# One output tile in three indirect transfers of 256 columns, and 30 identity matmuls at the start in place of 36

## Chip, cores and metric

The kernel runs on one core of a Trainium2 chip. The metric is the device time of one execution in microseconds (us); of several executions the median is given. The core has five engines that work side by side and meet at semaphores: TensorE (PE, matrix multiply; its weight loads are shown as PEld), VectorE (DVE), ScalarE (ACT), GpSimd (POOL) and SyncE (SP), and 16 DMA engines that move bytes between the chip's main memory and the on-chip memories.

## What is computed

Three stages follow one another. Attention over 2 batches, 12 heads, 448 positions and 64 columns per head gives 896 tokens of 768 columns. A mixture of 8 experts then sends each token through the one expert that its logits choose. Last comes a dense part, and it alone matters for the end of the kernel.

```python
def _moe2_ref(x, w1, w2, w3, w_out):
    h = np.maximum(np.maximum(x @ w1, x @ w2), x @ w3)
    return (h @ w_out).astype(np.float32)

def reference(...):
    x = attention(q, k, v)                     # (896, 768)
    x = _moe_ref(x, expert_emb, tau, w1, w2)   # one expert of 8 for each token
    return _moe2_ref(x, moe2_w1, moe2_w2, moe2_w3, moe2_w_out)   # (896, 768), float32
```

## The kernel before, in words

The order of the instructions on each engine is the order in which the program writes them; a framework puts in the semaphore waits that its view of the data needs. Every float32 product is made of three matmuls on two halves of each operand (`mm3`, lines 974 to 977).

**The start.** Lines 99 to 101 build the identity matrix `ident` and its 16-bit copy `identb` on POOL. Line 700 loads the keys and queries of the first head pair, and lines 703 to 705 run 36 matmuls of `identb` with itself (128 columns each) into a bank `warm` that nobody reads. Then the attention schedule begins: the keys `kt` of a pair are scaled on DVE (line 479), the scores go to PE (line 500), a mask is added by matmul (line 506), the row maximum is taken on DVE (line 510) and the exponential on ACT (line 517).

**The middle.** The tokens are sorted by expert, so that blocks of 128 rows use one expert's weights. `sorted_table2` (lines 970 to 972), which runs at the end of slot 1 (the second block of rows), inverts the sort with 16 small matmuls into a bank `ix` and casts seven columns of it into the integer table `sidx`. Column t of `sidx` holds, for each of the 128 rows of output tile t, the row of `out` that it belongs to.

**The end.** Seven output tiles of 128 rows and 768 columns are made in the loop over t (line 1102). Each has two parts n: the first 384 columns and the last 384, for the last tile 512 and 256 (line 1104). For each part 18 matmuls fill a bank `po`; ACT copies the first part into the tile `ob` (line 1110) and DVE the second (line 1112). After both, line 1113 scatters the whole tile with one indirect DMA that POOL issues; each row goes to the row of `out` that `sidx` names:

```python
nc.gpsimd.indirect_dma_start(out=out, out_offset=bass.IndirectOffsetOnAxis(ap=sidx[:, t:t + 1], axis=0), in_=ob, in_offset=None)
```

The buffers for `ob` alternate between two pools (line 1103). Line 1154 is the end of the program, where SP waits for all semaphores and the engines meet.

Of the kernel before, what the change touches and what calls it, by code (L numbers as in the profile page):

```python
# [10 lines left out]
I32 = mybir.dt.int32  # L11
AF = mybir.ActivationFunctionType
ALU = mybir.AluOpType
# [23 lines left out]
def kernel(  # L37
# [15 lines left out]
    nc = tc.nc  # L53
    B, H, S, D = 2, 12, 448, 64
    N, DM = out.shape
    E = emb.shape[0]
    P = 128
# [8 lines left out]
    const = ctx.enter_context(tc.tile_pool(name="const", bufs=1))  # L66
# [18 lines left out]
    def bank(tag, name, bufs=None):  # L85
        return ps.tile([P, 512], F32, tag=tag, name=name, bufs=bufs)

    V = nc.vector
# [175 lines left out]
    def mm3(o, lh, ll, rh, rl, first, last):  # L264
        nc.tensor.matmul(o, lhsT=lh, rhs=rh, start=first, stop=False)
        nc.tensor.matmul(o, lhsT=lh, rhs=rl, start=False, stop=False)
        nc.tensor.matmul(o, lhsT=ll, rhs=rh, start=False, stop=last)
# [199 lines left out]
    held = {}  # L467
# [233 lines left out]
    er, es, esq, table = embed(eb)  # L701
    consts(eb)
    warm = bank("h", "warm", 1)
    for n in range(36):
        nc.tensor.matmul(warm[:, :P], lhsT=identb, rhs=identb, start=True, stop=True)
    load(1)
    loadv(0)
# [144 lines left out]
    def invert(ns):  # L852
        ix = held["ix"] = bank("a", "ix")
        for c in range(NB):
            for t in range(2):
                nc.tensor.matmul(ix[:, :ns], lhsT=A[:, c], rhs=pay[:, t, c, :ns], start=(c + t == 0), stop=(c + t == NB))
# [90 lines left out]
    }  # L947

    sidx = const.tile([P, NB - 1], I32, name="sidx")

    def sorted_table():
        TT(rks[:, 4:], rks[:, 4:], padv[:TB].unsqueeze(1).to_broadcast([TB, 4, E]), ALU.subtract)
        TT(pre8, tri, n8.unsqueeze(1).to_broadcast([P, E, E]), ALU.mult)
        red(tb8, pre8)
        TT(ro, rks, tb8[:TB].unsqueeze(1).to_broadcast([TB, NB, E]), ALU.add)
        TT(ro, ro, oh, ALU.mult)
        red(rr, ro)
        TT(ge, rr.unsqueeze(2).to_broadcast([TB, NB, 6]), k128[:TB, 1:7].unsqueeze(1).to_broadcast([TB, NB, 6]), ALU.is_ge)
        red(sl, ge)
        V.scalar_tensor_tensor(out=jj, in0=sl, scalar=-128.0, in1=rr, op0=ALU.mult, op1=ALU.add)  # L960
        s7 = sel[:, :, :7]
        TT(s7, sl.unsqueeze(2).to_broadcast([TB, NB, 7]), i14[:TB, :7].unsqueeze(1).to_broadcast([TB, NB, 7]), ALU.is_equal)
        TT(pay[:, 0, :, :7], s7, bval[:TB].unsqueeze(2).to_broadcast([TB, NB, 7]), ALU.mult)
        V.tensor_scalar(out=pay[:, 1, :, :7], in0=s7, scalar1=pval[:TB], scalar2=None, op0=ALU.mult)
        onehot(0, 8)
        TT(flg, flg, tabf[:, NS:2 * NS], ALU.mult)
        red(tabf[:, 0:1], flg, ALU.max)
        V.tensor_copy(out=tabi[:, 3 * NS:], in_=tabf[:, 0:1])

    def sorted_table2():  # L970
        invert(7)
        V.tensor_copy(out=sidx, in_=held["ix"][:, :7])

    def mm3(o, lh, ll, rh, rl, first, last):
        nc.tensor.matmul(o, lhsT=lh, rhs=rh, start=first, stop=False)  # L975
# [13 lines left out]
    def rest_hint(i, *engines):  # L989
        tc.mark_branch_hint_location(f"rest{i}", (rest["n"] + (NS - i)) // 16, engines=engines)  # L990

    hooks = {(1, 0): sorted_table, (1, 1): sorted_table2, (5, 1): rest_load}
    for i in range(7, NS):
        hooks[i - 1, 0] = lambda i=i: rest_hint(i, ET.PE, ET.Pool, ET.SP)
# [63 lines left out]
    for m in range(KD):  # L1058
        t0 = [do.tile([P, S], F32, tag=f"t0{b}", name=f"t0{b}", bufs=1) for b in range(2)]
        wraw[m] = None  # L1060
        for a in range(3):
# [12 lines left out]
            else:  # L1074
                c = a - 1
# [26 lines left out]
    for t in range(N // P):  # L1102
        ob = (do, io_p)[t % 2].tile([P, DM], F32, tag="ob", name="ob")
        w = 512 if t == N // P - 1 else 384
        for n, (c0, c1) in enumerate(((0, w), (w, DM))):
            pb = bank("ab"[n], f"po{n}")[:, :c1 - c0]
            for k in range(KD):
                mm3(pb, hh[k // 3][:, k % 3, t * P:(t + 1) * P], hl[:, k, t * P:(t + 1) * P], woh[k][:, c0:c1], wol[k][:, c0:c1], k == 0, k == KD - 1)
            if n == 0:
                nc.scalar.copy(out=ob[:, :c1], in_=pb)  # L1110
            else:
                nc.vector.tensor_copy(out=ob[:, c0:], in_=pb)  # L1112
        nc.gpsimd.indirect_dma_start(out=out, out_offset=bass.IndirectOffsetOnAxis(ap=sidx[:, t:t + 1], axis=0), in_=ob, in_offset=None)  # L1113


_INS = ["q", "k", "v", "moe_expert_emb", "moe_tau", "moe_w1", "moe_w2", "moe2_w1", "moe2_w2", "moe2_w3", "moe2_w_out"]
# [42 lines left out]
```

## Time and profile before

| | |
|---|---|
| median of 3 runs | 478.21 us (477.86 to 478.9) |
| profiled execution, its own time | 477.87 us |
| its span (first to last instruction) | 476.2 us |
| PE busy | 462.1 us, 97% of the span |
| DVE, ACT, POOL busy | 322.7, 267.4, 81.0 us |

The span is what the trace shows; some 1.7 us of the execution lie around it. Times in a trace are counted from the start of the span. An engine's busy time says how much it did and not whether anybody waited for it; what bounds the end is read from the chain of work that ended last and from the instructions near that end.

### The profile page before, as it was taken

The page shows a single profiled execution, that of the slowest core. Times are in us where ns is not written, and L with a number is a line of the kernel's source. Part 1 is how long each engine was busy: PE and PEld are TensorE (multiplying, and loading weights), DVE is VectorE, ACT ScalarE, POOL GpSimd, SP SyncE. Part 2 cuts the span into 40 slices and gives each one's busy share as a digit, 9 for nine tenths or more (in the row PEclk, how much of TensorE's full clock was granted, in tenths as well). Part 3 has the DMA queues.
Part 4 walks back from the last instruction along what each step waited for, and adds up shares of the span by engine and source line. Part 5 has one row for each costly group of instructions (what it writes and reads, how often), then busy time and mean ns, then how long its engine had stood idle before and what let it go on. Part 6 is the DMA issues. An engine that isn't in the chain of part 4 may idle for free. (4 is left out here: it accounts for less than half of the span.)

```text
span 476.2 us, 9239 instructions
## 1 busy us (share of the span) xinstructions
PE 462.1 (97%) x3158; PEld 410.6 (86%) x3158; DVE 322.7 (68%) x650; ACT 267.4 (56%) x560; POOL 81.0 (17%) x103
## 2 busy tenths in 40 slices
PE   8999999899999999999999999999999999999994
PEld 6787768688899998998998987899999999999993
DVE  4999999968444895111977945898988979740000
ACT  6898979867726895234988955444435344310000
POOL 4868474620010000000000000000000000001111
PEclk9999999999999999999999999999999999999999
DMA  8734229441158890119799805754435220000111
GB/s 270 248 123 151 74 63 409 189 132 47 35 179 321 295 355 13 34 54 376 258 343 347 350 2 187 290 181 145 139 127 200 89 111 1 1 0 34 66 67 66
DMA packets 18173, 75.85 MB, mean 159 GB/s; under 512 B 2360, under 2 KB 5432, under 8 KB 18112
## 3 DMA queue, kind: packets, MB, share of 16 engines
q1 hardware_dynamic: 15408, 65.05, 38.3%
q0 software_dynamic: 2400, 9.83, 5.5%
q8 instruction: 26, 0.43, 0.4%
q10 hardware_dynamic: 304, 0.25, 0.2%
q14 instruction: 35, 0.29, 0.2%
HBM read 69.62 MB, written 5.51 MB: 158 GB/s over the span
## 5 line engine op out<-in xcount | busy, mean ns | idle before, releaser
L975 PE MATMUL pm<-x2h,dwh 128*128 128x448 f32 x204 | 75.1, 368 | 0.0
L976 PE MATMUL pm<-x2l,dwh 128*128 128x448 f32 x204 | 75.0, 368 | 0.0
L977 PE MATMUL pm<-x2h,dwl 128*128 128x448 f32 x204 | 74.6, 366 | 0.0
L981 PE MATMUL l<-w2h,hh 128*128 128x384 f32 x160 | 54.9, 343 | 0.7 <-ACT hh L207 0.7
L242 DVE TENSOR_TENSOR w1l<-raw,w1h 128x768 fp32r<-128x768 f32 x40 | 36.0, 950 | 27.8 <-PE l L981 20.5
L981 PE MATMUL l<-w2l,hh 128*128 128x384 f32 x160 | 53.7, 336 | 0.2 <-DVE w2l L262 0.2
L981 PE MATMUL l<-w1h,xhp 128*128 128x512 f32 x109 | 43.8, 402 | 0.0
L981 PE MATMUL l<-w1l,xhp 128*128 128x512 f32 x109 | 42.7, 392 | 0.0
L975 PEld LDWEIGHTS pm<-x2h,dwh 128*128 128x128 f32 x204 | 38.2, 187 | 3.9
L977 PEld LDWEIGHTS pm<-x2h,dwl 128*128 128x128 f32 x204 | 38.3, 188 | 3.7
L517 ACT ACTIVATE prb<-pss,sm 128x64 f32<-128x64 f32 (+6 forms) x84 | 39.2, 492 | 4.1 <-DVE sm L510 3.0
L174 ACT CAST dwh<-dt_t 128x768 fp32r<-128x768 f32 (+1 forms) x20 | 15.5, 773 | 46.2 <-DVE dt_t L173 46.1
L976 PEld LDWEIGHTS pm<-x2l,dwh 128*128 128x128 f32 x204 | 38.3, 188 | 3.4
L1113 POOL DMA_INDIRECT out_dram<-ob,sidx x7 | 6.8, 978 | 198.2 <-DVE ob L1112 198.2
L527 POOL TENSOR_SCALAR prb<-prb,sm 128x64 f32<-128x64 f32 (+6 forms) x38 | 36.0, 964 | 20.8 <-DVE sm L523 19.8
L198 POOL DMA_INDIRECT xrp<-xd,idx x11 | 11.3, 1028 | 152.9 <-PE xtp L216 143.2
L981 PE MATMUL l<-w2h,hl 128*128 128x384 f32 x160 | 36.3, 336 | 0.1
L242 DVE TENSOR_TENSOR w2l<-raw,w2h 128x768 fp32r<-128x768 f32 x40 | 35.1, 946 | 0.0
L204 DVE TENSOR_TENSOR hl<-htp,hh 128x512 fp32r<-128x512 f32 x17 | 11.7, 689 | 31.8 <-ACTq L351 17.8
L510 DVE TENSOR_REDUCE sm<-pss 128x1 f32<-128x128 f32 (+6 forms) x84 | 29.9, 411 | 3.5 <-PE pss L506 3.0
L241 ACT CAST w2h<-raw 128x768 fp32r<-128x768 f32 x40 | 30.5, 839 | 2.3 <-SPq L351 1.6
L241 ACT CAST w1h<-raw 128x768 fp32r<-128x768 f32 x40 | 31.7, 854 | 0.0
(255 smaller groups left out, 1023.9 us busy)
## 6 DMA issues: line engine op xcount, KB each, us to landing
raw<-in_moe_w_dram SPq DMA_DIRECT2D x48, 768.0 KB, 6.3
rawd<-in_moe_w_dram SPq DMA_DIRECT2D x18, 768.0 KB, 4.9
rawd<-in_moe_w_out_dram SPq DMA_DIRECT2D x6, 768.0 KB, 4.4
vr<-in_v_dram SPq DMA_DIRECT2D x12, 256.0 KB, 3.7
kt<-in_k_dram SPq DMA_DIRECT2D x12, 224.0 KB, 3.9
xd<-x2T POOLq DMA_DIRECT2D x12, 224.0 KB, 3.4
qt<-in_q_dram SPq DMA_DIRECT2D x11, 224.0 KB, 3.5
qt<-in_q_dram ACTq DMA_DIRECT2D x1, 224.0 KB, 4.0
```

The costliest lines, as they stand in the source:

```text
L174: nc.scalar.copy(out=hi[:, c0:c1], in_=f)
L198: nc.gpsimd.indirect_dma_start(out=xrp, out_offset=None, in_=xd if i else xd[0:S], in_offset=bass.IndirectOffsetOnAxis(ap=idx[:, i:i + 1] ...
L204: nc.vector.tensor_tensor(out=lo, in0=ps_ap, in1=hi, op=ALU.subtract)
L241: nc.scalar.copy(out=hi[:, sl], in_=r[:, sl])
L242: nc.vector.tensor_tensor(out=lo[:, sl], in0=r[:, sl], in1=hi[:, sl], op=ALU.subtract)
L510: nc.vector.tensor_reduce(out=sms[p][:, 0, SC[i]:SC[i] + 1], in_=held["s", p, g][:, SO[i]:SO[i] + 64 * (i + 1)], axis=AX.X, op=ALU.max, ne ...
L517: nc.scalar.activation(out=prb[p % 2][:, poff[i]:poff[i] + n], in_=ps[:, SO[i]:SO[i] + n], func=AF.Exp, bias=sm[:, 0, SC[i]:SC[i] + 1], sc ...
L527: eng.tensor_scalar(out=r, in0=r, scalar1=sms[p][:, 2, SC[i]:SC[i] + 1], scalar2=None, op0=ALU.mult)
L975: nc.tensor.matmul(o, lhsT=lh, rhs=rh, start=first, stop=False)
L976: nc.tensor.matmul(o, lhsT=lh, rhs=rl, start=False, stop=False)
L977: nc.tensor.matmul(o, lhsT=ll, rhs=rh, start=False, stop=last)
L981: nc.tensor.matmul(o, lhsT=a, rhs=b, start=first and n == 0, stop=last and n == len(ops) - 1)
```

## The change

The warm-up loop issues 30 matmuls. `sorted_table2` makes, beside `sidx`, a second integer table `sidx3` of three columns: three times the row number of the last tile, plus 0, 1 and 2. With `out` seen as 2688 rows of 256 columns, these are the rows at which the three thirds of an output row begin. The scatter moves into the loop over n: tiles 0 to 5 are still written whole after their second part; of the last tile two transfers of 256 columns follow its first part (512 columns) and one its second part.

```diff
-    for n in range(36):
+    for n in range(30):
         nc.tensor.matmul(warm[:, :P], lhsT=identb, rhs=identb, start=True, stop=True)
...
     sidx = const.tile([P, NB - 1], I32, name="sidx")
+    sidx3 = const.tile([P, 3], I32, name="sidx3")
...
     def sorted_table2():
         invert(7)
         V.tensor_copy(out=sidx, in_=held["ix"][:, :7])
+        for c in range(3):
+            V.tensor_scalar(out=sidx3[:, c:c + 1], in0=held["ix"][:, 6:7], scalar1=3.0, scalar2=float(c), op0=ALU.mult, op1=ALU.add)
...
-        nc.gpsimd.indirect_dma_start(out=out, out_offset=bass.IndirectOffsetOnAxis(ap=sidx[:, t:t + 1], axis=0), in_=ob, in_offset=None)
+            if t == N // P - 1:
+                for c in (2,) if n else (0, 1):
+                    nc.gpsimd.indirect_dma_start(out=out.rearrange("n (c d) -> (n c) d", c=3), out_offset=bass.IndirectOffsetOnAxis(ap=sidx3[:, c:c + 1], axis=0), in_=ob[:, 256 * c:256 * c + 256], in_offset=None)
+            elif n:
+                nc.gpsimd.indirect_dma_start(out=out, out_offset=bass.IndirectOffsetOnAxis(ap=sidx[:, t:t + 1], axis=0), in_=ob, in_offset=None)
```

## Rows read from the trace of the kernel before

**Rows 1.** The page: busy time, share of the span and instructions of each engine.
```profile
PE 462.1 (97%) x3158; PEld 410.6 (86%) x3158; DVE 322.7 (68%) x650; ACT 267.4 (56%) x560; POOL 81.0 (17%) x103
```

**Rows 2.** The chain that ended last, its end: start, length, engine, line.
```profile
470.36 0.51 issue
470.87 1.19 POOLq L1154
```

**Rows 3.** Timeline of the tail: start, length, engine, line, [idle before, releaser].
```profile
467.74 0.59 ACT L1110 COPY ob<-po 128x512 f32<-128x512 f32 x1 [6.76 <-PE po L977]
...
469.53 0.28 PE L977 MATMUL po<-woh,h2l 128*128 128x256 f32 x1
469.90 0.42 DVE L1112 COPY ob<-po 128x256 f32<-128x256 f32 x1 [5.71 <-PE po L977]
471.09 0.97 POOL L1113 DMA_INDIRECT out_dram<-ob,sidx  x1 [5.17 <-DVE ob L1112]
```

**Rows 4.** Line 1113 from 465 to 471 us: records, first and last start, landing time.
```profile
L1113 POOLq EVENT_SEMAPHORE  x2: 17/1181/2345, 468.0 to 468.0; - x2
L1113 POOL DMA_INDIRECT out_dram<-ob,sidx x1: 970/970/970, 465.0 to 465.0; - x1
...
DMA to landing us min/median/max: 3.0/3.0/3.0
```

**Rows 5.** Line 1113 over the span, seven scatters: from issue to landing.
```profile
DMA to landing us min/median/max: 3.0/3.0/4.1
```

**Rows 6.** Timeline of POOL, attention output written to `xd`; then line 594's landing times.
```profile
103.22 0.71 POOL L594 DMA_DIRECT2D xd<-x2T  x1 [4.22 <-ACT x2T L475]
105.54 0.71 POOL L594 DMA_DIRECT2D xd<-x2T  x1 [1.61 <-ACT x2T L475]
...
DMA to landing us min/median/max: 2.7/2.8/3.4
```

**Rows 7.** Slices of 0.2 us at the end: ..., PEclk, DMA share, GB/s.
```profile
472.60:472.80 0.20, 0.00 (x0) 0.00 (x0) 0.00 (x0) 0.00 (x0) 0.00 (x0) 1.00 1.16 492
...
473.40:473.60 0.20, 0.00 (x0) 0.00 (x0) 0.00 (x0) 0.00 (x0) 0.00 (x0) 1.00 0.46 184
```

**Rows 8.** Line 1154, 470 to 477 us: records, ns min/median/max, first and last start.
```profile
L1154 SPq EVENT_SEMAPHORE  x13: 17/28/28, 474.1 to 476.1; - x13
...
L1154 POOLq DRAIN  x3: 40/115/4480, 470.9 to 475.9; - x3
```

**Rows 9.** Timelines of POOL and PE at a gather of slot 6.
```profile
190.90 0.95 POOL L198 DMA_INDIRECT xrp<-xd,idx  x1 [17.83 <-PE xtp L216]
191.85 0.20 POOL L303 COPY glast<-gs 128x1 f32<-128x1 f32 x1
...
189.81 0.82 PE L216 MATMUL xtp<-ident,xrp 128*128 128x128 f32 x6
```

**Rows 10.** Timeline of DVE around `sorted_table2`.
```profile
140.98 0.17 DVE L972 CAST sidx<-ix 128x7 int32<-128x7 f32 x1 [0.80 <-DVEq L351]
148.79 0.96 DVE L242 TENSOR_TENSOR w1l<-raw,w1h 128x768 fp32r<-128x768 f32 x1 [7.64 <-PE l L981]
```

**Rows 11.** Timeline of the start: PE, PEld and DVE.
```profile
1.79 4.02 PE L705 MATMUL warm<-identb 128*128 128x128 bf16 x36 [1.79 <-POOL identb L101]
...
4.60 0.39 DVE L479 TENSOR_SCALAR kt<-kt 128x448 f32<-128x448 f32 x1 [2.96 <-DMA kt<-in_k_dram]
5.74 0.31 PEld L500 LDWEIGHTS pss<-kt,qt 64*64 64x64 f32 x8 [0.20 <-DVE kt L479]
...
7.36 2.94 DVE L510 TENSOR_REDUCE sm<-pss 128x1 f32<-128x448 f32 x8 [1.69 <-PE pss L506]
```

**Rows 12.** Score matmuls by form, from 5.7 to 6.0 us, then from 7.2 to 7.5 us.
```profile
L500 PE MATMUL pss<-kt,qt 64*64 64x448 f32 x2 | 1.0, 991 | 0.0
...
L500 PE MATMUL pss<-kt,qt 64*64 64x448 f32 x2 | 0.6, 587 | 0.0
```

## The prediction, on record before the changed kernel ran

> **What bounds the kernel now.** I read the page first: PE is busy in 97% of the span and no other engine in more than 68% [rows 1]. So an edit counts only if it shortens or lengthens PE's chain, or what hangs before its start and after its end. Both parts of the change sit there: the identity matmuls come ahead of PE's first useful work, and the scatter comes behind its last matmul. The end of the chain of waits ends on POOL's queue and not on PE [rows 2], so I next read the tail in order of time. ACT copies the first 512 columns of the last tile from 467.74 to 468.33; PE's last matmul starts at 469.53; DVE copies the other 256 columns until 470.32; POOL's scatter starts at 471.09 and takes 0.97 us, to 472.06 [rows 3]. The bytes move from about 472.6 to 473.5 [rows 7], SP sees the scatter land at 474.1 [rows 8], and the span ends at 476.2. So 6.6 us lie between PE's last start and the end, and only some 0.9 us of it moves bytes.
>
> The next view is line 1113's own records, because they say what a scatter waits for. POOL's two semaphore records of the last tile both start at 468.0, and the scatter of the tile before started at 465.0 and landed 3.0 us later, so at 468.0 [rows 4]. That means POOL stood at the last tile's scatter until the previous scatter had landed, although the previous one reads the other `ob` buffer. Today this costs nothing, because DVE's copy comes 2.3 us later. I asked whether this is a rule of POOL's DMA queue: two writes into `xd`, to different places, were issued at 103.22 and 105.54, 2.32 us apart, while such a write takes 2.7 us or more to land, and the second one's releaser is ACT [rows 6]. So writes to different places don't wait for each other and scatters into `out` do. A scatter's target is the whole of `out`, since its rows are known only at run time, and the new view of 2688 rows is the whole of `out` too.
>
> **The scatter in three, step by step.** Removed: one transfer of 768 columns. Added: three of 256 columns on the same queue, with the same target. By [rows 4] the second waits until the first has landed and the third until the second has. The price of each step:
>
> - From its last wait to its start. The scatter of before started 0.77 us after DVE's copy ended (470.32 to 471.09) [rows 3], of which 0.51 is issue [rows 2]. A gather with a single wait started 0.27 us after the last transpose that it waits for (189.81 + 0.82 = 190.63 to 190.90) [rows 9]. The bounds are 0.27 and 0.77. I take 0.77, because it is the same line with the same kind of waits.
> - From start to landing. Of the seven scatters the median took 3.0 us and the longest 4.1 [rows 5]. 0.9 us of the last one is bytes [rows 7]; a third of the bytes takes 0.3, which leaves 2.4. The 0.97 us on POOL stays, since there are still 128 indices. The bounds are 2.4 and 3.0 (nothing saved); I take 2.4.
> - The first transfer's start: the landing at 468.0 plus 0.77, against ACT's end at 468.33 plus 0.27 = 468.6. I take 468.75; the bounds are 468.6 and 468.33 + 0.77 = 469.1.
>
> The sum: first 468.75, landed 471.15; second 471.92, landed 474.32; third 475.09, landed 477.49. Before, the landing was at 474.1, so +3.4 us. With all low bounds: 468.6 + 3 x 2.4 + 2 x 0.27 = 476.34, +2.2. With all high bounds: 469.1 + 3 x 3.0 + 2 x 0.77 = 479.64, +5.5. By then DVE's copy (470.32) has long ended, so the third transfer waits for the second alone. What stands behind the landing (SP's row of waits, the drains, 2.1 us to the end) moves along with it. POOL's own drain ran 4.48 us from 470.9 to 475.4 [rows 8]; if it goes by the end of POOL's last issue rather than by the landing, the shift is 475.09 + 0.97 - 472.06 = +4.0, inside the bounds. Nothing else is queued behind POOL there.
>
> The Trainium skill, DMA: Bandwidth & Descriptors, section "Rules for kernel authors", speaks against the change: many small transfers should be coalesced into one, as below 64 KB one pays mostly overhead. Here the row has 3.0 us for a transfer of 384 KB, and each third has 128 KB. By that page's fit (section "Anatomy of one DMA — SWDGE (gpsimd) path": 2.0 us plus bytes over 436 GB/s) a third would cost 2.3 us, an estimate, in place of my 2.4, and the sum would be +3.1.
>
> **The table sidx3.** Three more DVE instructions of one column from the bank `ix`. The cast beside them took 0.17 us, so some 0.5 us, from 141.15 to 141.65. DVE's next record starts at 148.79 after 7.64 us of idleness that ended with a PE matmul [rows 10]: that idle time hides them. Bounds: 0, and 0.5 us if something waited on DVE there. I take 0. Tiles 0 to 5 issue the same scatter at the same point: 0.
>
> **Six identity matmuls fewer.** 36 of them start between 1.79 and about 5.5 us, 0.106 us apart. For 128 columns that is the lower of TensorE's two levels (1.2 GHz), though the page's clock column shows no change at the start. Six make 0.64 us, so the last would start at about 4.87. The first score's weight load came at 5.74, some 0.24 us after the last identity matmul's start [rows 11]; so now at 5.1. It needs the scaled keys, ready at 4.60 + 0.39 = 4.99 [rows 11], so PE doesn't stand still. But the first scores of 448 columns took 991 ns and the same form 587 ns at 7.2 us [rows 12]: PE was still on the lower level when they began and had risen soon after. If the rise comes at the same time, scores that start 0.64 us earlier run that much longer at half speed and gain half: 0.32 us. The row maximum that follows on DVE had waited 1.69 us for PE [rows 11], so the gain passes on to DVE and ACT. Bounds: 0.64 gained (the rise moves along), and 0.8 lost (the rise comes so much later that the scores to 7.25 us, 1.5 us of PE, run at half speed throughout). I take -0.32, since PE works through without a gap in both kernels.
>
> **The sum.** +3.4 - 0.3 = +3.1 us. On the profiled execution, 477.87 us with a span of 476.2, that gives 481.0; the median of the runs, 478.21, lies 0.34 above it, so 481.3 us. Bounds: 478.2 + 2.2 - 0.6 = 479.8 and 478.2 + 5.5 + 0 = 483.7.
>
> **The rivals.**
>
> 1. The transfers don't wait for each other (not slower). It decides at one point: whether the wait that [rows 4] shows is put in between transfers whose columns are disjoint. Then POOL issues two from 468.75 back to back (a copy followed the gather at 191.85 with no gap [rows 9]) until 470.7, the third starts at 471.09 as before, and lands 0.6 us earlier with its third of the bytes. With the start's 0.32: 478.2 - 0.9 = 477.3 us; with 0.64 it would be 477.0. For it: the three columns of `sidx3` name different rows of the new view. Against it: the rows of the seven scatters of before are different too, and they waited. Chance 0.10. The Trainium skill's same page and section "Rules for kernel authors" says that a DMA issued early, with its semaphore waited on late, has its fixed cost overlapped; by that rule this rival would hold, but here the trace shows the wait ahead of the issue.
>
> 2. DVE's copy waits too. If the framework sees `ob` as one thing, DVE may write its last 256 columns only after both first transfers have read theirs, so from 474.32: copied by 474.74, third start 475.51, landed 477.91, +3.8 us in place of +3.4. 481.7 us. For it: nothing but the possibility; ACT and DVE wrote their parts of `ob` in order anyhow. Chance 0.08.
>
> 3. The clock rises later. The forecast's tail with 0.8 lost at the start instead of 0.3 gained: 482.4 us. Chance 0.04.
>
> That the change does what it says only in part is in the forecast: of the two transfers that are to run under the last matmuls only the first does (468.75 to 471.15), the second starts after them.
>
> **How the numbers follow.** The forecast, 481.3, has a chance of 0.78, the rivals 0.10, 0.08 and 0.04. Rivals 2 and 3 lie within the forecast's own bounds. The range runs from 479.6 to 483.6, which leaves out rival 1 (0.10) and some 0.07 of slower landings, as the 4.1 us of one of seven [rows 5]. This kernel's measurement can tell about 0.2%, 0.96 us, from no change. Slower: forecast and rivals 2 and 3, less a little for low bounds together, 0.89. Rival 1 divides at its -0.9: within 0.2% 0.07, faster 0.04.
>
> **What would show it.** In the profile after: three POOL scatters at the end, each starting 0.3 to 0.8 us after the landing of the one before, about 3.2 us apart (rival 1: 1 us apart); landing times of 2.4 us; DVE's copy near 470.0 (rival 2: behind the second landing); the span's end some 2.1 us after the last landing. At the start, 30 identity matmuls and the first weight load near 5.1 us, with the first row maximum 0.3 us earlier than 7.36. The prediction would be wrong if the three starts are a microsecond apart, or if the start loses what 36 matmuls kept.

## The result, and the profile after

The changed kernel takes 481.78 us (median of six runs, 481.48 to 483.86), the kernel before, run beside it, 478.03 us (six runs, 476.92 to 478.9). The ratio is 1.0088 [1.0072, 1.0104], so it is 4.2 us slower by the ratio, and 3.75 us by the two medians. Forecast were 481.3 us, a range of 479.6 to 483.6, and slower with a chance of 0.89. The profiled execution took 481.48 us with a span of 479.8; before it was 477.87 and 476.2, so +3.6 us on both.

The page of the kernel after: the first line answers to [rows 1] (PE is as busy as it was), the second is the end of the chain, by engine.

```profile
PE 462.0 (96%) x3152; PEld 409.9 (85%) x3152; DVE 323.0 (67%) x653; ACT 267.2 (56%) x560; POOL 82.9 (17%) x105
...
DMA 1%; issue 1%; POOLq 0%
```

The tail of the kernel after, which answers to [rows 3]: start, length, engine, line, [idle before, releaser]. Line numbers are now 3 higher up to the copies and 5 to 7 higher behind them: L1118 issues the thirds, L1120 the whole tiles, L1113 is ACT's copy, L1115 DVE's, L1161 the end.

```profile
468.31 0.59 ACT L1113 COPY ob<-po 128x512 f32<-128x512 f32 x1 [6.76 <-PE po L980]
...
469.31 0.97 POOL L1118 DMA_INDIRECT out_dram<-ob,sidx  x1 [2.81 <-ACT ob L1113]
...
470.10 0.28 PE L980 MATMUL po<-woh,h2l 128*128 128x256 f32 x1
470.47 0.42 DVE L1115 COPY ob<-po 128x256 f32<-128x256 f32 x1 [5.71 <-PE po L980]
472.00 0.97 POOL L1118 DMA_INDIRECT out_dram<-ob,sidx  x1 [1.71 <-DMA out_dram<-ob,sidx]
475.18 0.97 POOL L1118 DMA_INDIRECT out_dram<-ob,sidx  x1 [2.21 <-DMA out_dram<-ob,sidx]
```

Three scatters, 2.69 and 3.18 us apart, and what released the second and third is the landing (DMA) of the one before. The second one's data, ACT's 512 columns, had been ready since 468.90, for 3 us. DVE's copy comes 0.1 us after PE and waits for no transfer. The chain that ended last has the same story in order of time (start, length, what):

```profile
465.53 0.97 DMA out_dram<-ob,sidx
466.50 2.60 issue
469.10 0.02 POOLq L1118
469.12 0.19 issue
469.31 2.42 DMA out_dram<-ob,sidx
471.73 0.27 issue
472.00 2.42 DMA out_dram<-ob,sidx
474.42 0.02 issue
474.44 0.02 POOLq L1118
474.46 0.50 issue
474.96 1.20 POOLq L1161
```

From PE's last matmul (470.10) to the end of the span (479.78) are 9.68 us; before, 6.64 (469.53 to 476.17, [rows 3] and the span). The transfers therefore cost 3.0 us of the 3.6. The bytes are not what takes the time; slices of 0.4 us of the kernel after (..., PEclk, DMA share, GB/s) show one busy slice for the first third:

```profile
470.40:470.80 0.40, 0.00 (x0) 0.00 (x0) 0.33 (x1) 0.00 (x0) 0.00 (x0) 1.00 0.00 0
470.80:471.20 0.40, 0.00 (x0) 0.00 (x0) 0.10 (x1) 0.00 (x0) 0.00 (x0) 1.00 0.87 317
471.20:471.60 0.40, 0.00 (x0) 0.00 (x0) 0.00 (x0) 0.00 (x0) 0.00 (x0) 1.00 0.04 10
```

Of the 2.42 us, 1.5 pass before the first byte and some 0.4 after the last. The Trainium skill, DMA: Bandwidth & Descriptors, section "Anatomy of one DMA — SWDGE (gpsimd) path", has 2.0 us plus bytes over 436 GB/s, which makes an estimate of 2.3 us for a third; the trace has 2.42, 0.12 more. The same section lays most of the 2.0 us to the receipt behind the last byte; here most of it lies ahead of the first byte.

### The profile page after: what moved, and what is told of

Same layout as the page of the kernel before. It is cut to its first block, busy times and chain, and to the rows that moved or that the text cites. A ratio compares the mean times of both kernels' runs of the same rounds, so it can differ in the third digit from the quotient of the medians.

```text
span 479.8 us, 9233 instructions
## 1 busy us (share of the span) xinstructions
PE 462.0 (96%) x3152; PEld 409.9 (85%) x3152; DVE 323.0 (67%) x653; ACT 267.2 (56%) x560; POOL 82.9 (17%) x105
## 5 line engine op out<-in xcount | busy, mean ns | idle before, releaser
L1120 POOL DMA_INDIRECT out_dram<-ob,sidx x6 | 5.9, 980 | 193.3 <-DVE ob L1115 193.3
```

## The experiments

The theory after the result: POOL's scatters into one tensor stand one behind the other's landing, and that alone makes the kernel slower. The rivals: (R1) they stand behind each other because one queue carries them, whatever they write; (R2) the table `sidx3`, priced at nothing, has a part in it; (R3) the 30 identity matmuls cost at the start.

### The scatter alone

The kernel before with the three transfers and the table, and 36 identity matmuls left as they were.

```diff
+    sidx3 = const.tile([P, 3], I32, name="sidx3")
+        for c in range(3):
+            V.tensor_scalar(out=sidx3[:, c:c + 1], in0=held["ix"][:, 6:7], scalar1=3.0, scalar2=float(c), op0=ALU.mult, op1=ALU.add)
...
+            if t == N // P - 1:
+                for c in (2,) if n else (0, 1):
+                    nc.gpsimd.indirect_dma_start(out=out.rearrange("n (c d) -> (n c) d", c=3), out_offset=bass.IndirectOffsetOnAxis(ap=sidx3[:, c:c + 1], axis=0), in_=ob[:, 256 * c:256 * c + 256], in_offset=None)
...
```

> The scatter's part alone: three transfers and the table sidx3, but 36 identity matmuls as before. Theory (each transfer waits for the landing of the one before): the three scatters start 0.25 to 0.8 us after the landing before them, about 2.7 to 3.2 us apart; from the start of ACT's last copy to the end of the span 11.4 us where the kernel before had 8.4; time +3.0 us, about 481.0. Rival (the start is what cost the time, by a clock that rises later): about 478. A third reading: the three more DVE instructions of sidx3 move DVE's code, and DVE stands 2 us behind the branches at about 291 us as it did in the changed kernel; then the first sums of the dense part start about 1.4 us late here too.

Measured: 482.1 us against 477.37, ratio 1.0097 [1.0084, 1.0111], +4.6 us. From the last matmul (470.45) to the span's end (480.11) again 9.66 us, +3.0. So the whole loss is in the scatter and its table, but only 3.0 of the 4.6 in the tail: something ahead of it takes the rest. The kernel after, with 30 identity matmuls in place of 36, was 4.2 slower than before and not 4.6; these two intervals overlap.

### The identity matmuls alone

```diff
-    for n in range(36):
+    for n in range(30):
```

> The start's part alone: 30 identity matmuls, one scatter per tile as before. Theory: the first score's weight load at 5.0 us in place of 5.7 and no idle PE ahead of it; 0.3 us faster, up to 1.0 where TensorE comes up to its higher level early: 477.2 to 477.9. Rival (the clock rises later with fewer matmuls): the first scores of 448 columns take 990 ns as before and those at 6.3 us too, and the time is 0.8 us longer, 478.8. By the reading that the three DVE instructions of sidx3 cost the 1.4 us at 291 us, DVE doesn't stand there in this kernel.

Measured: 477.5 us against 477.37, ratio 0.9995 [0.9986, 1.0004]. The interval takes in the 0.32 us of the forecast and no change; R3 as a loss of more than 0.2 us is excluded. Why it is not a clean 0.3 is told with the start, below.

### Three targets in place of one

Each third goes to a scratch tensor of its own, so no two of the last transfers write the same one. The rows of the last tile are not written to `out`; `sidx` serves as the index, and there is no new table.

```diff
+    scr = [dram.tile([N, 256], F32, name=f"scr{c}") for c in range(3)]
...
+            if t == N // P - 1:
+                for c in (2,) if n else (0, 1):
+                    nc.gpsimd.indirect_dma_start(out=scr[c], out_offset=bass.IndirectOffsetOnAxis(ap=sidx[:, t:t + 1], axis=0), in_=ob[:, 256 * c:256 * c + 256], in_offset=None)
...
```

> The last tile's three transfers go to three scratch tensors in memory in place of the output (so the last tile's 128 rows of the output are not written); 36 identity matmuls. Theory (the wait comes from the shared target): no wait for a landing between the three; the first two start 1.0 us apart, the third 0.77 us after DVE's copy or behind the second, and the last landing comes 0.6 us earlier than in the kernel before: 477.4 us. Rival (POOL's queue runs one transfer at a time whatever its target): the starts are 2.7 us apart and the time is 481, as with the changed kernel.

Measured: 477.43 us, ratio 1.0002 [0.9991, 1.0013]. POOL's timeline in this kernel:

```profile
468.04 0.97 POOL L1116 DMA_INDIRECT scr<-ob,sidx  x1 [2.67 <-ACT ob L1111]
469.31 0.97 POOL L1116 DMA_INDIRECT scr<-ob,sidx  x1 [0.30 <-issue]
470.59 0.97 POOL L1116 DMA_INDIRECT scr<-ob,sidx  x1 [0.30 <-issue]
```

Same engine, same queue, same sizes, and the starts are 1.27 us apart with no landing between them. R1 falls: it is the shared target that puts the landings in a row. The wait for a landing is a semaphore wait of POOL's, in a record ahead of the transfer ([rows 4], and 474.44 in the chain above) or in the transfer's own instruction, so it is put in by the framework. No run leaves it out with the target shared. The tail is 6.2 us (468.96 to 475.2), 0.4 below before; the time of the runs shows no gain. Expected were 0.6: the last landing is 0.5 earlier (4.0 us behind PE's last matmul in place of 4.5), as the smaller transfer saves 0.6 us, but the third issue stands behind the second (0.97 + 0.30 us) and starts 0.83 us after DVE's copy, no sooner than the whole tile's did. Even without the waits the split hardly pays.

### Three scatters without the new tile and without DVE's part

The row numbers are made on POOL from `sidx`, in a tile that is dead by then. The scatter is as in the run of the scatter alone, and there are 36 identity matmuls.

```diff
+    sidx3 = eq.bitcast(I32)[:, :3]
...
+        for c in range(3):
+            nc.gpsimd.tensor_scalar(out=sidx3[:, c:c + 1], in0=sidx[:, 6:7], scalar1=3.0, scalar2=float(c), op0=ALU.mult, op1=ALU.add)
...
```

> Three scatters of the last tile with neither a new tile nor new DVE instructions: the row numbers of the thirds are made on POOL, from sidx, in a tile that is no longer used; 36 identity matmuls. Theory: only the tail of the change is left, so +3.0 us against the kernel before (480.4), and neither a loss per slot nor DVE's stand at 291 us. Rival (the slots' loss belongs to the three scatters): 482, as with the scatters alone.

Measured: 481.48 us against 477.95, ratio 1.0076 [1.006, 1.0092], +3.6 us. POOL's timeline:

```profile
468.07 0.97 POOL L1118 DMA_INDIRECT out_dram<-ob,eq  x1 [3.17 <-ACT ob L1113]
471.21 0.97 POOL L1118 DMA_INDIRECT out_dram<-ob,eq  x1 [2.17 <-issue]
474.39 0.97 POOL L1118 DMA_INDIRECT out_dram<-ob,eq  x1 [2.21 <-DMA out_dram<-ob,eq]
```

The starts are 3.14 and 3.18 us apart, and the tail is 10.4 us (468.50 to 478.94), +3.8, as against +3.0 above. The table's tile is gone and the transfers still stand in a row, so R2 has no part in the tail. The gap between a landing and the next start is 0.76 and 0.79 us here (a third lands 2.38 us after its start), while the second scatter of the changed kernel had 0.27. What differs is what the instruction waits for last: here its own wait is on POOL (which made `eq`), and the landing is a semaphore record of its own ahead of it. In the changed kernel's chain the same shows: behind the record at 474.44 come 0.50 us of issue and then more, 0.76 us in all from the landing at 474.42 to the start, while the landing at 471.73 is followed by 0.27 us and the start.

### The last two copies exchanged

That reading of the gap was put to a test on the kernel before, with its one scatter of the last tile: DVE copies the first 512 columns and ACT the last 256, so that the copy that ends last is ACT's.

```diff
-            if n == 0:
-                nc.scalar.copy(out=ob[:, :c1], in_=pb)
+            if (n == 0) != (t == N // P - 1):
+                nc.scalar.copy(out=ob[:, c0:c1], in_=pb)
             else:
-                nc.vector.tensor_copy(out=ob[:, c0:], in_=pb)
+                nc.vector.tensor_copy(out=ob[:, c0:c1], in_=pb)
```

> The kernel before with the engines of the last tile's two copies exchanged: DVE copies the first 512 columns, ACT the last 256. One scatter per tile, 36 identity matmuls. In the changed kernel the second transfer started 0.25 us after the landing it waited for and the third 0.75 us after its. Theory: 0.5 us of the 0.75 is work that POOL does on the instruction before it looks at the instruction's own wait, and of several waits that on ACT is the instruction's own; then the last scatter starts 0.25 to 0.3 us after ACT's copy in place of 0.77 us after DVE's, the tail from PE's last matmul to the end is 0.5 us shorter, and the time is 0.5 us less (477.3 against 477.8). Rival (the 0.77 us are paid after any wait): the same time as before.

Measured: 477.05 us against 477.55, ratio 0.9988 [0.9979, 0.9997]. ACT's copy (ended at 470.35) is followed by the scatter at 470.62, 0.27 us later, where [rows 3] have 0.77; the tail is 6.1 us (469.62 to 475.7), 0.55 shorter. Of this 0.50 is the gap, and 0.05 that ACT copies the 256 columns in 0.37 us where DVE took 0.42.

```profile
469.98 0.37 ACT L1110 COPY ob<-po 128x256 f32<-128x256 f32 x1 [8.91 <-PE po L977]
```

```profile
470.62 0.97 POOL L1113 DMA_INDIRECT out_dram<-ob,sidx  x1 [4.60 <-ACT ob L1110]
```

So both bounds of the prediction's first term, 0.27 and 0.77, exist, and which one holds depends on whether the last event is the instruction's own wait or a record ahead of it. In [rows 4] one of POOL's two records lasted 2345 ns from 468.0, to 470.3: it was DVE's copy that stood in the record. What POOL does in the half microsecond behind such a record, no run shows.

### Two transfers in place of three

As the run with the dead tile, with two halves of 384 columns.

```diff
-        w = 512 if t == N // P - 1 else 384
+        w = 384
...
+            if t == N // P - 1:
+                nc.gpsimd.indirect_dma_start(out=out.rearrange("n (c d) -> (n c) d", c=2), out_offset=bass.IndirectOffsetOnAxis(ap=sidx3[:, n:n + 1], axis=0), in_=ob[:, c0:c1], in_offset=None)
...
```

> The last tile in two transfers of 384 columns, one after each part, with parts of 384 and 384 columns; row numbers made on POOL in a tile no longer used, 36 identity matmuls. Theory (one landing per transfer): the first starts about 0.75 us after the landing of the tile before and lands 2.5 us later, the second starts 0.75 us after that and lands 2.5 us later: about 0.5 us later than the single scatter of before, +0.5 us (478.3 against 477.8), where three transfers cost +3.0. Rival (each further transfer costs the same 1.5 us): +1.5, 479.3.

Measured: 478.41 us against 477.55, ratio 1.0017 [1.0009, 1.0026], +0.8 us; the tail is 7.4 us (468.76 to 476.17), +0.8. The chain's end in this kernel:

```profile
464.28 2.97 DMA out_dram<-ob,sidx
...
467.27 0.02 POOLq L1117
...
467.34 0.04 POOLq L1117
467.38 0.73 issue
468.11 2.53 DMA out_dram<-ob,eq
...
470.77 0.51 issue
```

The first half waits for the tile before it and the second for the first half, each 2.53 us; one landing less in the row than with thirds gives back 3.0 us of the 3.8. It is 0.3 us more than expected, mostly by the gaps: 0.86 us from each landing to the next start in place of 0.75, as two records and not one stand ahead of each transfer.

### The table, its tile and its instructions apart

Two runs of the kernel before, each with one half of what the table brings: the tile alone, written once by POOL and never read; and three more casts on DVE into `sidx`, with no new tile.

```diff
+    sidx3 = const.tile([P, 3], I32, name="sidx3")
+    nc.gpsimd.memset(sidx3, 0)
```

> The kernel before with the tile sidx3 (3 integers per partition) beside sidx, set to zero by one POOL instruction and never read; no more DVE instructions, one scatter per tile, 36 identity matmuls. The three traces with sidx3 lost about 0.15 us in each of the slots from 130 to 290 us and won 1.3 us back in the dense part from 360 to 425 us; the two traces without it did neither. Theory A (the tile shifts every tile that is laid out after it, and TensorE reads those tiles at another pace): the same loss per slot and the same gain in the dense part here, and no stand of DVE at 291 us; net 0 (-0.2 to +0.2). Theory B (it is the three DVE instructions): this kernel runs like the kernel before, slot by slot.

```diff
         V.tensor_copy(out=sidx, in_=held["ix"][:, :7])
+        for c in range(3):
+            V.tensor_copy(out=sidx[:, c:c + 1], in_=held["ix"][:, c:c + 1])
```

> The kernel before with three more DVE casts behind the cast that makes sidx, which write the same values into sidx again; no new tile, one scatter per tile, 36 identity matmuls. Theory (the three DVE instructions move DVE's code): DVE stands 2.2 us behind the branches at 291 us, and the first sums of the dense part are 1.4 us late; about +1.4 us, 478.8. Rival (the stand comes with the tile or with the three scatters): DVE goes on 0.2 us after the branch as in the kernel before, and the time is the same, 477.4.

Measured: the tile 478.94 us against 477.95, ratio 1.0015 [1.0003, 1.0028], +0.7 us; the casts 478.4, ratio 1.0007 [0.9994, 1.0021], +0.3. The first is a small loss, the second can't be told from none by time, but both can be seen in the traces. To read them, a second profile of the kernel before was taken.

> The kernel before once more, for a second trace. The first scores of 448 columns at 5.75 us take 990 ns or 590 ns, depending on when TensorE comes up to its higher level in this execution (6.6 us in the first trace, 5.7 in two others with 36 identity matmuls): then the start of the kernel varies by up to 0.4 us by itself. DVE goes on 0.2 us after the branch at 291 us.

It took 477.52 us with a span of 475.8. The gathers of POOL, one for each slot of the expert part, show the pace of PE (each is released by PE's transposes). First the second profile of the kernel before, then the tile alone, then the kernel after:

```profile
153.00 0.94 POOL L198 DMA_INDIRECT xrp<-xd,idx  x1 [13.71 <-PE xtp L216]
...
265.64 0.97 POOL L198 DMA_INDIRECT xrp<-xd,idx  x1 [17.61 <-PE xtp L216]
```

```profile
152.99 0.94 POOL L198 DMA_INDIRECT xrp<-xd,idx  x1 [13.80 <-PE xtp L216]
...
266.51 0.97 POOL L198 DMA_INDIRECT xrp<-xd,idx  x1 [17.75 <-PE xtp L216]
```

```profile
152.79 0.95 POOL L198 DMA_INDIRECT xrp<-xd,idx  x1 [13.78 <-PE xtp L216]
...
266.31 0.97 POOL L198 DMA_INDIRECT xrp<-xd,idx  x1 [17.75 <-PE xtp L216]
```

Six slots take 112.64, 113.52 and 113.52 us: with the tile each is 0.15 us longer, though nobody reads it. The kernel after has the tile without POOL's instruction that sets it to zero, and loses as much: that instruction is not the cause. In the dense part the order turns. PE reaches it 1.0 us late with the tile (292.21 us for 291.19), and the first output matmul only 0.2 late; first before, then the tile alone:

```profile
425.58 0.34 PE L975 MATMUL po<-woh,h2h 128*128 128x384 f32 x1
```

```profile
425.79 0.34 PE L977 MATMUL po<-woh,h2h 128*128 128x384 f32 x1
```

So the net loss of this trace is 0.2 us, less than the 0.7 of the runs; its execution (477.79 us) was one of the fastest of its twelve.

The casts show in another place. DVE's first work behind the last branch of the expert part (line 279), in the second profile of the kernel before, then with the casts, then in the kernel after:

```profile
290.75 0.62 DVE L279 TENSOR_SCALAR y<-l,glast 128x384 f32<-128x384 f32 x1 [4.99 <-PEq L1011]
```

```profile
293.13 0.62 DVE L279 TENSOR_SCALAR y<-l,glast 128x384 f32<-128x384 f32 x1 [6.98 <-ACT x2h L203]
```

```profile
293.70 0.62 DVE L279 TENSOR_SCALAR y<-l,glast 128x384 f32<-128x384 f32 x1 [7.12 <-ACT x2h L203]
```

DVE's last branch record (line 1011, 1013 and 1014 in turn) starts at 290.3, 290.6 and 291.3; then it goes on after 0.4 us in the kernel before, and after 2.5 and 2.4 us with three more instructions on DVE. All four profiles of kernels with the three instructions on DVE have this stand (DVE idle for 6.9 to 7.1 us ahead of line 279), and none of the ten others has it (4.9 to 5.1 us), with the tile or without. PE feels it where its matmuls read DVE's `x2l`: the first six of them took 1.48 us before and 2.62 after (and 2.48 with the casts alone, 1.46 with the row numbers made on POOL). The first row is of the second profile of before, the second of after.

```profile
294.62 1.48 PE L981 MATMUL pm<-x2l,dwh 128*128 128x448 f32 x6
```

```profile
295.44 2.62 PE L984 MATMUL pm<-x2l,dwh 128*128 128x448 f32 x6
```

The three instructions bring the stand, then, and the tile does not; what DVE waited for behind the branch has no record. The Trainium skill, Runtime: NRT & Kernel Launch, section "Instruction fetch mechanics", says that a taken branch whose target lies outside the pages held makes the engine wait for a fetch. That could fit, but the traces don't settle it: an 8 KB transfer of the instruction queue starts 0.4 us behind this branch record in the kernel after (at 291.69, ended by 292.2, while DVE goes on at 293.5), but also in the second profile of before (at 290.73, when DVE had already gone on), and the profile doesn't say for which engine it is.

### A larger tile

The last run asked whether the tile's odd size matters: 64 bytes in each partition in place of 12. The edit is shown against the run with the tile alone.

```diff
-    sidx3 = const.tile([P, 3], I32, name="sidx3")
+    sidx3 = const.tile([P, 16], I32, name="sidx3")
```

> The kernel before with one tile more of 64 bytes per partition (16 columns of int32, written once by POOL, never read), in place of the 12 bytes of the run with the small tile alone. That run showed gathers of the expert slots 18.92 us apart where the kernel before has 18.77, and a dense part that gave some 0.8 us back. Theory A: what counts is that 12 bytes put every later tile off a boundary that 64 bytes keep; then the gathers stand 18.77 us apart again, the dense part keeps its pace, and the time is that of before (ratio 1.000, within 0.001). Theory B: what counts is any shift of the later tiles, or the memset on POOL; then the gathers stand 18.92 us apart, some 1.2 us are lost by 280 us and some 0.8 us given back after it, ratio 1.001 to 1.002.

Measured: 480.39 us against 477.32, ratio 1.0065 [1.0053, 1.0078], +3.1 us, from a tile that nobody reads.

```profile
154.00 0.94 POOL L198 DMA_INDIRECT xrp<-xd,idx  x1 [13.87 <-PE xtp L216]
...
268.16 0.97 POOL L198 DMA_INDIRECT xrp<-xd,idx  x1 [17.86 <-PE xtp L216]
```

Both theories missed. Six slots take 114.16 us, 0.25 us more for each than before, and the dense part gives back only some 0.4 us. It is no matter of a boundary of 64 bytes. That a tile nobody reads changes PE's pace, and that another size changes it by another amount, is shown by the two runs. That it does so by moving the tiles allocated behind it is the likely reading, but no run shows where they lie; which operand it is, and by what rule, is open. The matmuls themselves are slower: those of 512 columns in the slots start 0.232 us apart with either tile and 0.229 in the kernel before (medians), those of 384 columns 0.175 us with the tile of 64 bytes and 0.173 in the other two, with the clock column at 1.00 in all three; that column shows 1.00 at the start too, where PE runs at half pace, but a fall to the lower level would double these spacings, and they grew by 1%. Of the 2.9 us by which this trace's last matmul is late against the second profile of before, 1.0 is there at the first gather (0.8 of it from the start, with the first row maximum at 7.76 us; see next), 1.5 come in the six slots, 0.8 behind them, and 0.4 is given back.

### The start once more

> The changed kernel once more, for a second trace of it. If DVE's stand of 2.2 us behind the branches at 291 us comes from where its code lies, it is here again, and the first sums of the dense part are late by the same 1.4 us; if it varies from execution to execution, it is gone. The three scatters: the same 2.7 and 3.2 us apart, landings of 2.4 us. The time at which the first scores run at the higher level may differ (4.7 us in the first trace).

Measured: 482.26 us, span 480.6. PE's timeline at the start, in the first profile of the kernel after and then in this one:

```profile
1.80 3.23 PE L705 MATMUL warm<-identb 128*128 128x128 bf16 x30 [1.80 <-POOL identb L101]
5.00 0.99 PE L500 MATMUL pss<-kt,qt 64*64 64x448 f32 x12
...
6.28 0.99 PE L500 MATMUL pss<-kt,qt 64*64 64x448 f32 x12
```

```profile
1.79 3.38 PE L705 MATMUL warm<-identb 128*128 128x128 bf16 x30 [1.79 <-POOL identb L101]
5.10 1.37 PE L500 MATMUL pss<-kt,qt 64*64 64x448 f32 x12
...
7.34 0.99 PE L500 MATMUL pss<-kt,qt 64*64 64x448 f32 x12 [0.68 <-DVE sm L510]
```

Twelve scores take 0.99 us when they run wholly on the higher of TensorE's two levels (2.4 GHz), and 1.37 when the rise comes between them. In the first profile it had come before them (the last two identity matmuls start 0.057 us apart, those before them 0.106), in the second it came among them, and in the first trace of before their first two were still slow [rows 12]. So the rise moves from one execution to the next, with 30 matmuls as with 36, and DVE's first row maximum moves with it: 7.36 [rows 11] and 6.95 in the two profiles of the kernel before, 6.22 and 6.70 in those of the kernel after, and 7.76 in the run with the larger tile. In the second profile of after PE then lost time again: the second pair's scores began at 7.34, where 6.6 would have followed the mask, because their queries, issued at 1.7, landed only at 7.2. In the first profile they also began later than the mask allowed, 0.36 us behind its start (5.92 to 6.28) where it was 0.19 in the second profile of before (6.65 to 6.84); the landing that would show why is not in that trace. (The row names DVE's row maximum as the releaser, but in no other execution did these scores wait for it: in the second profile of before they started at 6.84, ahead of the first maximum at 6.95.) With a like rise (between 5.5 and 5.7 us in both, as the spacing of the identity matmuls and the times of the scores show), the 30 matmuls gain 0.34 us: the row maximum stands at 6.95 in the second profile of before and at 6.61 in the run with 30 matmuls alone.

```profile
6.95 2.35 DVE L510 TENSOR_REDUCE sm<-pss 128x1 f32<-128x448 f32 x6 [1.44 <-PE pss L506]
```

```profile
6.61 2.81 DVE L510 TENSOR_REDUCE sm<-pss 128x1 f32<-128x448 f32 x7 [1.21 <-PE pss L506]
```

Over the ten profiles of kernels with 36 matmuls its median is 6.96 us (6.49 to 7.76), over the four with 30 it is 6.66 (6.22 to 6.79): 0.3 us between the middles, and more than that from one execution to the next.

### What beats both

The exchanged copies and the 30 matmuls together.

> The exchanged copies and 30 identity matmuls together. Theory: 0.5 us from the tail and 0.3 us on average from the start, so 0.8 us less than the kernel before, 477.0 against 477.8. Rival (either is hidden or given back): within 0.3 us of the kernel before. Where the second pair's queries land later than 6.2 us, the start gives back what it gained.

Measured: 476.49 us against 477.55, ratio 0.9982 [0.9972, 0.9992], 0.9 us faster than the kernel before, with the scatter 0.28 us behind ACT's copy and a tail of 6.1 us (468.58 to 474.7).

## Why the prediction was right, and where it was not

The account of the profiled kernel after against the second profile of the kernel before, whose spans differ by 4.0 us. "Late by" is the difference at that place, "new" what came since the place above:

| place | before | after | late by | new |
|---|---|---|---|---|
| first gather | 153.00 | 152.79 | -0.21 | -0.2 |
| last gather | 265.64 | 266.31 | +0.67 | +0.9 |
| first output matmul | 425.58 | 426.50 | +0.92 | +0.25 |
| last matmul | 469.18 | 470.10 | +0.92 | 0 |
| end of the span | 475.82 | 479.78 | +3.96 | +3.04 |

The third step is DVE's stand (about +1.1) and the last slot (+0.15) less what the dense part gives back (-1.0).

- **The mechanism.** Right: each third stands behind the landing of the one before, and by the run with three targets because they share one. Rival 1 is answered by that run too: what decides is the tensor and not the columns. Rival 2 is wrong; DVE's copy began 0.1 us after PE. Rival 3 did not come: the rise moves whatever the count, and in the two profiles of after the first row maximum was earlier than in either of before.
- **From the last wait to the start (0.77 for each).** Mis-sized for one of the three: the gaps were 0.76, 0.27 and 0.76. "The same line with the same kind of waits" did not hold for the second, which waits for nothing but the landing. The first start, 469.31, is the landing of the tile before (465.53 + 3.02 = 468.55) plus 0.76, just as worked out from [rows 4].
- **From start to landing (2.4).** Right: 2.41 to 2.42 for all three.
- **The tail's sum.** +3.4 was forecast, +3.0 came: the second gap took 0.5 off, and small differences put 0.1 back. The stretch behind the last landing moved along almost unchanged (477.6 to 479.8, 2.2 us, where 2.1 was forecast).
- **The table sidx3 (0, at most 0.5).** Wrong. DVE's 7.64 us of idleness [rows 10] did hide the three instructions where they run. The cost came elsewhere: the stand behind a branch 150 us later, and the slower slots that come with the tile, some +2.1 us by the stand's end and -1.0 in the dense part, +1.1 in all in this trace. The step asked only what waits beside the new work, and not what else a new tile and new instructions change. By the runs the two halves gave 0.7 us (tile, 0.1 to 1.3 by the interval) and 0.3 (casts, -0.3 to 1.0). Why either costs anything is open.
- **Six identity matmuls (-0.32).** The size was right where the rise is alike (-0.34), though the runs with 30 matmuls alone can't tell it from none. The rise moves by more than that from one execution to the next, and the sentence that PE works through without a gap did not hold: in the second profile of after the second pair's scores stood 0.75 us for their queries, which 36 matmuls had covered, and in the first they were 0.17 us late.
- **The total.** 481.3 against 481.78. The forecast counted from the first profile of before, 477.87 us, and there +3.1 was forecast and +3.6 came: 0.4 less from the tail, 1.1 more from the table, and 0.2 less from the start, whose first gather is 0.56 us earlier than in that profile. It was right in sign and mechanism; that it was this close owes something to the errors' signs. By the ratio of the runs the change costs 4.2 us and not 3.1. The sum's upper bound (483.7) took the start at 0 though its own bound was 0.8 lost; 484.5 would have followed.

## What to carry to other kernels

In this program an indirect write waits for the one before it into the same tensor, whichever rows and columns they name: split such a write and each part pays a full landing, here 2.4 us for 0.5 us of bytes plus 0.27 to 0.86 us to the next start. Leave it whole; even over three tensors the split gained nothing by the time of the runs. Ahead of a last transfer, look at which event its instruction waits for itself: letting that be the one that comes last was worth 0.5 us here without any work saved. And test a new tile or a few instructions far from the critical path by a run that has them and nothing else, not by the idle time around them.

## What was not expected of the hardware

- A never-read tile of 12 bytes in each partition made the expert slots 0.8% slower (18.92 for 18.77 us) and one of 64 bytes 1.4% (19.03), with the dense part faster by 0.8 and 0.4 us of 134. The cause is open.
- Three more instructions on DVE made it stand 2.4 us, not 0.4, behind a branch 150 us later.
- POOL started an indirect transfer 0.27 to 0.28 us after the event where that was the instruction's own wait, and 0.76 to 0.86 us after it where a separate semaphore record took it. Two indirect transfers into different tensors, with no wait between them, started 1.27 us apart.
- The first row maximum, which follows the clock's rise, came between 6.22 and 7.76 us in the traces, and an input load issued at 1.7 us took up to 5.5 us to land.
